# Attention tiles hold two heads of both batches of a pair: products g evicted over 128 rows, products h over two halves of 64 rows

## The chip, the core and the metric

One core of a Trainium2 chip. The metric is the device time of one execution in microseconds; the kernel before ran three times, with a median of 1440.73 (1438.68 to 1441.16). A further execution was profiled. TensorE multiplies (its weight loads are PEld in the profile), VectorE (DVE) and ScalarE (ACT) read its results from PSUM, which has eight banks, GpSimd (POOL) works on on-chip memory only, and SyncE (SP) issues all DMAs, in order.

## What is computed

Attention with 32 memory slots per head, then two MoE-like layers without routing:

```python
a = softmax over the sequence of phi                      # batch 8, heads 8, seq 576, slots 32
k_m, v_m = a^T k, a^T v                                   # per head: 32 x 64
attn = softmax over the slots of (q k_m^T / 8);  out = attn v_m
x = out, heads side by side                               # 4608 tokens x 512
h = max(x w1, x w2, x w3);  x2 = h w_out                  # w: 512 x 768, w_out: 768 x 512
y = (sigmoid(x2 w_gate) * (x2 w_val)) w_out2              # 512 x 1536 twice, 1536 x 512
```

## The kernel before

Every product is done with operands split into a rounded upper part and a remainder, in three passes (`PASSES`: low by high, high by low, high by high), to keep the precision.

*Pairs.* The batches are taken two at a time: pair `p` of four holds batches `2p` and `2p+1`. Attention works on groups of four heads of one batch (16 groups, `n`), in stages `a0` to `a5`: maximum and exponential of phi, transposes on TensorE (L193, L194), `k_m` and `v_m` (L207), transposes of those (L227; `a3` leaves the transposed `v_m` in `VT`), scores (L245), softmax, and `a_split`, which leaves the weights of the slots, 4 heads x 32 = 128 rows by 576 tokens, high and low, in `AT[n]`.

*Products g and h.* The output of attention is never formed. Since `x w = attn (v_m w)`, `g_step` multiplies `v_m` into a piece of the weights, and `h_step` multiplies the attention weights into that. `j` runs over six blocks of 128 of the 768 columns, `hp` over the four pairs of heads, `w` over w1, w2, w3. One `g_step(p, j, hp)` takes two heads of *both* batches: 128 rows come out, 32 for each head and batch, by 3 x 128 columns. An `h_step` wants the four heads of one batch in 128 rows, so `g_step` writes each half of its 64 rows to another tile, `G[b, j, g]`: two copies by ScalarE (the high part, L356) and two subtractions by VectorE (the low part, called in `sub`, L73) of 64 x 384 each. In pair 0, where `hp` is 0, ScalarE copies the product to `gf` first and GpSimd subtracts. `h_step(p, j, u)` then does 288 tokens of one batch (`u` from 0 to 3: batch `u // 2`, half `u % 2`): 18 matmuls over 128 rows into three PSUM banks (L369), a copy and two maxima (L379 to L381), and the high and low parts of `h`.

*x2.* `x2_step` multiplies all six blocks of `h` with `wo1` (L392), copies the result to a tile `x` of three buffers and stores it in DRAM (`x2s`).

*Order.* A loop over `s` sets it: 24 steps of `g_step(p, j+1, u)` and `h_step(p, j, u)`, then 16 of `x2_step`, with the next pair's attention stages spread over them by the spacing `a_st`. Into pair 0 the conversion and splitting of the first layer's weights is strewn (`w_step`: L122 to L126, `w_split` L131), into pairs 0 and 1 the conversion of the second layer's (`b_step`), into pair 3 sums and splits of those (`t_steps`, tiles `tb`) and of the first rows of the second layer (`x_load`, `x_sums`, `x_split`: tiles `xf`, `xa`). A scheduler then moves instructions on each engine. The second layer (L690, L757) follows; the change doesn't touch it.

Of the kernel before, what the change touches and what calls it, by code (L numbers as in the profile page):

```python
# [18 lines left out]
def attn_moe_kernel(  # L19
# [20 lines left out]
    U = S // 2  # L40
# [22 lines left out]
    def f32(ap):  # L63
        return ap.bitcast(F32)
# [69 lines left out]

    A = {}

    def early(shape):

        t = low.tile([128, 2 * U], F32R, tag="h", name="early", bufs=4 * J)
        return f32(t[:, :shape[1]])  # L140

    def load_phi(n):
        st = A[n] = {"kv": [], "q": []}
        if n in (2, 3):
            st["phi"] = early([128, S])
        else:
            st["phi"] = att.tile([128, S], F32, tag="phi", name="phi", bufs=2)
        dma(st["phi"], phiT[n])

    def load_kv(n):  # L150
        for c in range(5):
            if n < 4:
                t = early([128, 512])
            else:
                t = att.tile([128, 512], F32, tag="kv", name="kv", bufs=7)
            if c < 4:
                dma(t, kvm[n, c])
            else:
                dma(t[:64], kvt[n])
            A[n]["kv"].append(t)  # L160

    def load_q(n, e):
        if (n, e) in ((0, 0), (0, 1)):
            t = early([128, S])
        else:
            t = att.tile([128, S], F32, tag="q", name="q", bufs=3)
        dma(t, qT[n, e])
        A[n]["q"].append(t)


# [50 lines left out]

    def a3(n):
        st = A[n]
        b, g = divmod(n, 2)
# [6 lines left out]
        if b % 2 == 0:  # L231
            VT[b // 2, g] = mid.tile([128, 2, 4, 64], F32R, tag="vt", name="vt", bufs=4)
        vt = VT[b // 2, g]
        src = p[:, 128:256].rearrange("p (h m) -> p h m", h=2)
        for h in range(2):
            x = 3 * h if b % 2 == 0 else 2 - h
            act.copy(vt[:, 0, x], src[:, h])
            sub(vec, vt[:, 1, x], src[:, h], f32(vt[:, 0, x]))

    def a4(n):  # L240
        st = A[n]
# [90 lines left out]
    PASSES = ((1, 0), (0, 1), (0, 0))  # L332

    def g_step(p, j, hp):
        g, e = divmod(hp, 2)
        if e == 0:
            for b in range(2):
                G[b, j, g] = mid.tile([128, 2, 384], F32R, tag=f"g{b}", name=f"g{b}", bufs=3 + b)
        ps = bank()
        vt, w = VT[p, g], WX.pop((j, hp))  # L340
        for n, (x, y) in enumerate(PASSES):
            pe.matmul(  # L342
                ps[:, :384],
                lhsT=vt[:, x, 2 * e:2 * e + 2].rearrange("p a m -> p (a m)"),
                rhs=w[:, y],
                start=(n == 0), stop=(n == 2),
            )
        yield
        src, eng = ps, vec
        if p == 0 and hp == 0:  # L350
            src, eng = mid.tile([128, 384], F32, tag="gf", name="gf", bufs=1), pool
            act.copy(src, ps[:, :384])
        for hf in range(2):
            r = slice(64 * hf, 64 * hf + 64)
            t = G[(hf + e) % 2, j, g]
            act.copy(t[r, 0], ps[r, :384])  # L356
            sub(eng, t[r, 1], src[r, :384], f32(t[r, 0]))

    H = {}

    def h_step(p, j, u):
        b, hf = divmod(u, 2)
        ps = [bank() for _ in range(3)]
        for w in range(3):
            n = 0
            for g in range(2):
                at = AT[2 * (2 * p + b) + g]
                for x, y in PASSES:
                    pe.matmul(  # L369
                        ps[w][:, :U],  # L370
                        lhsT=G[b, j, g][:, x, 128 * w:128 * w + 128],
                        rhs=at[:, y, hf * U:hf * U + U],
                        start=(n == 0), stop=(n == 5),
                    )
                    n += 1
        yield
        h = mid.tile([128, U], F32, tag="hf", name="hf", bufs=2)
        m = mid.tile([128, U], F32, tag="hm", name="hm", bufs=2)
        act.copy(h, ps[0][:, :U])  # L379
        vec.tensor_tensor(out=m, in0=ps[1][:, :U], in1=h, op=ALU.max)  # L380
        vec.tensor_tensor(out=m, in0=ps[2][:, :U], in1=m, op=ALU.max)  # L381
        t = low.tile([128, 2 * U], F32R, tag="h", name="h", bufs=4 * J).rearrange("p (two t) -> p two t", two=2)
        H[u, j] = t
        copy(vec if u == 0 else act, t[:, 0], m)
        sub(pool, t[:, 1], m, f32(t[:, 0]))

    def x2_step(p, u, d):
        ps = bank()
        n = 0
        for j in range(J):  # L390
            for x, y in PASSES:
                pe.matmul(  # L392
                    ps[:, :U],
                    lhsT=wo1_t[:, x, (d * J + j) * 128:(d * J + j) * 128 + 128],
                    rhs=H[u, j][:, y],
                    start=(n == 0), stop=(n == 3 * J - 1),
                )
# [169 lines left out]
    for p in range(NP):  # L567
# [63 lines left out]
        for s in range(NS + NX):  # L631
            if last and s == NS:
                mid.release()
                b1 = tc.alloc_tile_pool(name="b1", bufs=1, side="right", reuse_waits="tile")
            gens = []
            for k, n in atts.get(s, ()):
                if len(atts[s]) > 1:
                    run(stages[k](n))
                    load_ahead(k, n)
                else:  # L640
                    gens.append(stages[k](n))
            if s < NS:
# [225 lines left out]
```

## Time and profile before

| | us |
|---|---|
| median of three runs | 1440.73 |
| the profiled execution | 1442.94 |
| its span | 1440.4 |
| TensorE busy (x7864 matmuls) | 1351.1 |
| VectorE, ScalarE, GpSimd busy | 843.7, 582.8, 545.8 |
| products g (L342), 37.5 to 524.9 | 71.7 busy |
| products h (L369), 51.3 to 536.8 | 258.2 busy |
| x2 (L392), 161.0 to 575.0 | 159.3 busy |
| second layer, first matmul | 608.5 |

The span is the time from the first to the last instruction of the profiled execution; its own device time is 2.5 us longer. Products h of pair 0 stand from 51 to 161, of pair 1 from 215 to 298, of pair 2 from 345 to 423, of pair 3 from 468 to 537, each followed by that pair's x2.

### The profile page before, as it was taken

To read this page: it belongs to the slowest core of one execution; us is meant where nothing else is said; L and a number is where in the kernel's file an instruction comes from. 1 tells how busy PE (TensorE), PEld (TensorE's weight loads), DVE (VectorE), ACT (ScalarE), POOL (GpSimd) and SP (SyncE) were. 2 spreads that over 40 slices of the span, in tenths; PEclk is the share of its full clock that TensorE was granted. 3 is DMA by queue.
4 is the path that set the end of the run, shared out by engine and by line. 5 is a ranking of instruction groups with operands and counts; after the bars stand their busy time and mean duration, and the time that the engine had idled before them with its cause. 6 is when DMAs were issued, how large, how long until landed. Compare 5 with 4: busy or idle time off the path is not lost.

```text
span 1440.4 us, 22273 instructions
## 1 busy us (share of the span) xinstructions
PE 1351.1 (94%) x7864; PEld 1187.6 (82%) x7864; DVE 843.7 (59%) x1508; ACT 582.8 (40%) x1236; POOL 545.8 (38%) x480
## 2 busy tenths in 40 slices
PE   6578899999999999199999999999999999999998
PEld 3477788889999999088888888888888899999997
DVE  5999979987754872334545445544355544454454
ACT  6668657756553662332223222242212422132221
POOL 3666512341344677921128211182112721161111
PEclk8789999999999999599999999999999999999999
DMA  9578799977636967874456644565444666566651
GB/s 306 197 249 290 263 308 329 305 274 262 187 91 238 402 251 288 323 295 147 159 178 216 205 146 146 171 213 200 151 149 156 218 233 225 184 232 220 222 204 72
DMA packets 120045, 320.75 MB, mean 223 GB/s; under 512 B 13440, under 2 KB 29824, under 8 KB 119936
## 3 DMA queue, kind: packets, MB, share of 16 engines
q1 hardware_dynamic: 119936, 319.35, 65.0%
q8 instruction: 62, 1.02, 0.3%
q14 instruction: 47, 0.39, 0.1%
HBM read 253.23 MB, written 66.06 MB: 222 GB/s over the span
## 4 chain that ended last, share of the span: by engine, by line
PE 74%; DVE 7%; DMA 7%; ACT 4%; issue 4%; POOL 3%; SPq 0%; DVEq 0%; POOLq 0%; ACTq 0%
PE po L757 21%; PE px L690 16%; PE pz L690 10%; PE pv L690 10%; PE ps L369 8%; PE ps L392 5%; DMA raw<-wb_dram 2%; DMA raw<-wx_dram 2%; PE ps L342 2%; DVE g L73 2%; DVE ca L126 1%; POOL tb L73 1%; DVE ca L124 1%; POOL xa L73 1%; ACT g L356 1%
## 5 line engine op out<-in xcount | busy, mean ns | idle before, releaser
L73 POOL TENSOR_TENSOR gg<-gf,gg 128x512 fp32r<-128x512 f32 (+1 forms) x120 | 142.4, 1186 | 556.1 <-ACT gg L723 556.1
L757 PE MATMUL po<-wo,gg 128*128 128x512 f32 x1296 | 332.8, 395 | 1.0 <-POOL gg L73 1.0
L757 PEld LDWEIGHTS po<-wo,gg 128*128 128x128 f32 x1296 | 242.6, 188 | 55.2 <-POOL gg L73 1.3
L690 PE MATMUL px<-xa,tb 128*128 128x512 f32 (+1 forms) x1080 | 248.0, 371 | 33.2 <-DMA tb<-tbs 33.2
L369 PE MATMUL ps<-attn,g 128*128 128x288 f32 x1728 | 258.2, 303 | 20.9 <-POOL s L73 7.0
L369 PEld LDWEIGHTS ps<-attn,g 128*128 128x128 f32 x1728 | 245.4, 193 | 30.8 <-POOL s L73 7.3
L690 PEld LDWEIGHTS px<-xa,tb 128*128 128x128 f32 x1080 | 199.8, 189 | 63.0 <-issue 33.4
L769 DVE TENSOR_TENSOR acc<-po,acc 128x512 f32<-128x512 f32 x180 | 124.4, 691 | 202.7 <-PE po L757 202.5
L690 PE MATMUL pv<-xa,tb 128*128 128x512 f32 (+1 forms) x720 | 170.3, 369 | 0.0
L690 PE MATMUL pz<-xa,tb 128*128 128x512 f32 (+1 forms) x720 | 170.0, 369 | 0.0
L392 PE MATMUL ps<-h,wo 128*128 128x288 f32 x1152 | 159.3, 297 | 0.0
L392 PEld LDWEIGHTS ps<-h,wo 128*128 128x128 f32 x1152 | 155.7, 190 | 1.9 <-issue 0.8
L741 DVE TENSOR_TENSOR u<-pz,p 128x512 f32<-128x512 f32 (+1 forms) x120 | 76.3, 636 | 131.4 <-PE pz L690 127.0
L690 PEld LDWEIGHTS pz<-xa,tb 128*128 128x128 f32 x720 | 132.6, 188 | 19.6
L723 ACT CAST gg<-gf 128x512 fp32r<-128x512 f32 (+1 forms) x120 | 69.5, 579 | 193.3 <-DVE gf L719 137.1
L690 PEld LDWEIGHTS pv<-xa,tb 128*128 128x128 f32 x720 | 131.8, 188 | 18.7
L73 POOL TENSOR_TENSOR h<-hm,h 128x288 fp32r<-128x288 f32 x96 | 87.6, 916 | 140.1 <-ACT h L68 83.5
L713 ACT ACTIVATE sg<-sg 128x512 f32<-128x512 f32 (+1 forms) x90 | 53.1, 590 | 163.2 <-DVE sg L711 163.0
L73 DVE TENSOR_TENSOR g<-ps,g 64x384 fp32r<-64x384 f32 x180 | 99.2, 551 | 26.2 <-ACT g L356 22.8
L356 ACT CAST g<-ps 64x384 fp32r<-64x384 f32 x192 | 90.9, 474 | 43.1 <-DVE g L73 21.9
L73 POOL TENSOR_TENSOR xa<-xf,xa 128x512 fp32r<-128x512 f32 (+1 forms) x70 | 84.9, 1239 | 29.9 <-ACT xa L131 29.7
L342 PE MATMUL ps<-wx,vt 128*128 128x384 f32 x288 | 71.7, 359 | 9.6 <-DVE vt L73 3.4
(87 smaller groups left out, 1398.5 us busy)
## 6 DMA issues: line engine op xcount, KB each, us to landing
tb<-tbs SPq DMA_DIRECT2D x210, 512.0 KB, 3.9
wo<-wos SPq DMA_DIRECT2D x60, 512.0 KB, 4.9
wx<-wxs SPq DMA_DIRECT2D x72, 384.0 KB, 5.2
tbs<-tb SPq DMA_DIRECT2D x42, 512.0 KB, 5.2
raw<-wb_dram SPq DMA_DIRECT2D x48, 384.0 KB, 4.9
kv<-kvm_dram SPq DMA_DIRECT2D x48, 256.0 KB, 4.4
raw<-wx_dram SPq DMA_DIRECT2D x24, 384.0 KB, 3.6
wxs<-wx SPq DMA_DIRECT2D x24, 384.0 KB, 5.2
```

Of the source, the lines that this page charges most:

```text
L73: eng.tensor_tensor(out=o, in0=a, in1=b, op=ALU.subtract)
L124: vec.tensor_scalar(out=ai, in0=ai, scalar1=3, scalar2=None, op0=ALU.logical_shift_left)
L342: pe.matmul(ps[:, :384], lhsT=vt[:, x, 2 * e:2 * e + 2].rearrange("p a m -> p (a m)"), rhs=w[:, y], start=(n == 0), stop=(n == 2),)
L356: act.copy(t[r, 0], ps[r, :384])
L369: pe.matmul(ps[w][:, :U], lhsT=G[b, j, g][:, x, 128 * w:128 * w + 128], rhs=at[:, y, hf * U:hf * U + U], start=(n == 0), stop=(n == 5),)
L392: pe.matmul(ps[:, :U], lhsT=wo1_t[:, x, (d * J + j) * 128:(d * J + j) * 128 + 128], rhs=H[u, j][:, y], start=(n == 0), stop=(n == 3 * J - 1),)
L690: pe.matmul(ps[:, :half], lhsT=w[:, a, o:o + 128], rhs=x[:, k, c, :half], start=(first and n == 0), stop=(n == 5), skip_group_check=not first,
L713: act.activation(out=sg, in_=src, func=AF.Sigmoid)
L723: act.copy(t[:, 0, :half], gf)
L741: vec.tensor_tensor(out=u, in0=ps[:, :half], in1=E["p1", v], op=ALU.add)
L757: pe.matmul(ps, lhsT=GG[sc, j, c, h][:, x, 128 * m:128 * m + 128], rhs=WO[sc, j, h][:, y], start=(n == 0), stop=(n == 5),)
L769: vec.tensor_tensor(out=t, in0=ps, in1=t, op=ALU.add)
```

## The change

Attention groups are cut otherwise: group `n = 4p + hp` holds two heads of batch `2p` in rows 0 to 63 and the same two heads of batch `2p+1` in rows 64 to 127 (`source` says where they stand in the inputs, which keep their layout). The rows of attention weights, of `v_m` and of a product g are now in the same order, so `a3` copies `v_m` whole, and `g_step` evicts its 128 rows with one copy and one subtraction into one tile `G[j, hp]`, always by ScalarE and VectorE. An `h_step` now does one half of the tokens for both batches: 72 matmuls over 64 rows each, which alternate between the lower half of the rows (batch 0) and the upper (batch 1), into six PSUM banks. The `h` tiles hold both batches (576 columns), their upper part is always copied by ScalarE, and the number of h steps per `j` is two instead of four. Loads of phi, k and v come in two pieces per group, one for each batch; k and v in runs of 256 numbers instead of 512. `x` has two buffers instead of three.

```diff
+    def source(n, b):
+        p, hp = divmod(n, 4)
+        g, pr = divmod(hp, 2)
+        return 2 * (2 * p + b) + g, pr ^ b
...
-        dma(st["phi"], phiT[n])
+        for b in range(2):
+            m, pr = source(n, b)
+            dma(st["phi"][64 * b:64 * b + 64], phiT[m, 64 * pr:64 * pr + 64])
...
+            for b in range(2):
+                m, pr = source(n, b)
+                dma(t[:, :, 256 * b:256 * b + 256],
+                    kvm[m, c:c + 2, :, 256 * pr:256 * pr + 256].rearrange("c s x -> s c x"))
...
     def a3(n):
...
-        for h in range(2):
-            x = 3 * h if b % 2 == 0 else 2 - h
-            act.copy(vt[:, 0, x], src[:, h])
-            sub(vec, vt[:, 1, x], src[:, h], f32(vt[:, 0, x]))
+        vt = VT[n] = mid.tile([128, 2, 128], F32R, tag="vt", name="vt", bufs=8)
+        act.copy(vt[:, 0], p[:, 128:256])
+        sub(vec, vt[:, 1], p[:, 128:256], f32(vt[:, 0]))
...
     def g_step(p, j, hp):
...
-        src, eng = ps, vec
-        if p == 0 and hp == 0:
-            src, eng = mid.tile([128, 384], F32, tag="gf", name="gf", bufs=1), pool
-            act.copy(src, ps[:, :384])
-        for hf in range(2):
-            r = slice(64 * hf, 64 * hf + 64)
-            t = G[(hf + e) % 2, j, g]
-            act.copy(t[r, 0], ps[r, :384])
-            sub(eng, t[r, 1], src[r, :384], f32(t[r, 0]))
+        t = G[j, hp] = mid.tile([128, 2, 384], F32R, tag="g", name="g", bufs=8)
+        act.copy(t[:, 0], ps[:, :384])
+        sub(vec, t[:, 1], ps[:, :384], f32(t[:, 0]))
...
-    def h_step(p, j, u):
-        b, hf = divmod(u, 2)
-        ps = [bank() for _ in range(3)]
+    def h_step(p, j, hf):
+        ps = [[bank() for _ in range(2)] for _ in range(3)]
         for w in range(3):
             n = 0
-            for g in range(2):
-                at = AT[2 * (2 * p + b) + g]
+            for hp in range(4):
+                at = AT[4 * p + hp]
                 for x, y in PASSES:
-                    pe.matmul(
-                        ps[w][:, :U],
-                        lhsT=G[b, j, g][:, x, 128 * w:128 * w + 128],
-                        rhs=at[:, y, hf * U:hf * U + U],
-                        start=(n == 0), stop=(n == 5),
-                    )
+                    for b in range(2):
+                        r = slice(64 * b, 64 * b + 64)
+                        pe.matmul(
+                            ps[w][b][:, :U],
+                            lhsT=G[j, hp][r, x, 128 * w:128 * w + 128],
+                            rhs=at[r, y, hf * U:hf * U + U],
+                            start=(n == 0), stop=(n == 11),
+                        )
                     n += 1
         yield
-        h = mid.tile([128, U], F32, tag="hf", name="hf", bufs=2)
-        m = mid.tile([128, U], F32, tag="hm", name="hm", bufs=2)
-        act.copy(h, ps[0][:, :U])
-        vec.tensor_tensor(out=m, in0=ps[1][:, :U], in1=h, op=ALU.max)
-        vec.tensor_tensor(out=m, in0=ps[2][:, :U], in1=m, op=ALU.max)
...
-        copy(vec if u == 0 else act, t[:, 0], m)
+        m = mid.tile([128, 2, U], F32, tag="hm", name="hm", bufs=2)
+        for b in range(2):
+            act.copy(m[:, b], ps[0][b][:, :U])
+        for w in (1, 2):
+            for b in range(2):
+                vec.tensor_tensor(out=m[:, b], in0=ps[w][b][:, :U], in1=m[:, b], op=ALU.max)
...
+        act.copy(t[:, 0], m)
         sub(pool, t[:, 1], m, f32(t[:, 0]))
...
-        t = low.tile([128, U], F32, tag="x2", name="x2", bufs=3)
+        t = low.tile([128, U], F32, tag="x2", name="x2", bufs=2)
...
-                gens.append(h_step(p, j, u))
+                if u % 2 == 0:
+                    gens.append(h_step(p, j, u // 2))
```

What stands on TensorE in the middle of pair 2's products h, before: L342 is a product g, L369 products h (`g_` tiles are its weights), L193 and L194 transposes of attention.

```order
L342 MATMUL ps<-wx,vt 128x384 x3
L369 MATMUL ps<-attn,g_4776 128x288 x9
L193 MATMUL ps<-ident,et 128x128 x4
L194 MATMUL ps<-ident,et 64x128
L369 MATMUL ps<-attn,g_4890 128x288 x9
```

And in the changed kernel, from the end of pair 1's x2 (L407) into pair 2: L359 is g, L381 h, L219, L220 and L233 attention.

```order
L407 MATMUL ps<-h,wo_82 128x288 x90
L359 MATMUL ps<-wx,vt 128x384 x3
L381 MATMUL ps<-attn,g 128x288 x72
L219 MATMUL ps<-ident,et 128x128 x4
L220 MATMUL ps<-ident,et 64x128
L359 MATMUL ps<-wx,vt 128x384 x3
L233 MATMUL ps<-kv,es 32x128 x16
L233 MATMUL ps<-kvt,es 32x128 x4
```

The h matmuls, 64 rows each, now stand in one block of 72, with g, attention or x2, which use other tilings of the array, on both sides.

VectorE in pair 0 where the first maximum stands, before (`hm` is the maximum, `g_` a product g's low part, `ca` a weight's conversion in three steps):

```order
L126 SCALAR_TENSOR_TENSOR ca<-raw,ca 128x384
L125 ISA ca<-ca,cr 128x768
L73 TENSOR_TENSOR g_654<-ps,g_654 64x384
L380 TENSOR_TENSOR hm<-ps,hf 128x288
L271 TENSOR_SCALAR sm<-sm 128x18
```

The same place in the changed kernel:

```order
L73 TENSOR_TENSOR g<-ps,g 128x384
L124 TENSOR_SCALAR ca<-ca 128x384
L125 ISA ca<-ca,cr 128x768
L124 TENSOR_SCALAR ca<-ca 128x384
L126 SCALAR_TENSOR_TENSOR ca<-raw,ca 128x384
L125 ISA ca<-ca,cr 128x768
L126 SCALAR_TENSOR_TENSOR ca<-raw,ca 128x384
L394 TENSOR_TENSOR hm<-ps,hm 128x288
```

One subtraction of 128 rows stands where two of 64 stood, and 14 conversions (L126) are ahead of the first maximum instead of nine.

GpSimd at the end of pair 3's products h, before: `tb` are the second layer's weights, `xa` its rows.

```order
L73 TENSOR_TENSOR tb<-td,tb 128x512
L73 TENSOR_TENSOR tb<-tw,tb 128x512
L73 TENSOR_TENSOR tb<-two,tb 128x512 x2
L73 TENSOR_TENSOR h<-hm,h 128x288 x2
L73 TENSOR_TENSOR tb<-tw,tb 128x512
L73 TENSOR_TENSOR h<-hm,h 128x288
L73 TENSOR_TENSOR xa<-xf,xa 128x512
```

And in the changed kernel:

```order
L73 TENSOR_TENSOR tb<-td,tb 128x512
L73 TENSOR_TENSOR tb<-tw,tb 128x512
L73 TENSOR_TENSOR tb<-two,tb 128x512 x2
L73 TENSOR_TENSOR h<-hm,h 128x576
L73 TENSOR_TENSOR tb<-tw,tb 128x512
L73 TENSOR_TENSOR h<-hm,h 128x576 x6
L73 TENSOR_TENSOR xa<-xf,xa 128x512
```

All 37 pieces `tb` that stood among or ahead of pair 3's pieces of h still do, and 17 still follow; the last six pieces of h now come together.

More of the change, by code (lines that the diff above doesn't have):

```diff
@@ L135, in attn_moe_kernel, with early_tile, early @@
     A = {}
-    def early(shape):
-        t = low.tile([128, 2 * U], F32R, tag="h", name="early", bufs=4 * J)
-        return f32(t[:, :shape[1]])
+    halves = []
+    def early_tile():
+        return f32(low.tile([128, 4 * U], F32R, tag="h", name="early", bufs=2 * J))
+    def early(cols):
+        if not halves:
+            t = early_tile()
+            halves.extend((t[:, :2 * U], t[:, 2 * U:]))
+        return halves.pop(0)[:, :cols]
+    def source(n, b):
+        p, hp = divmod(n, 4)
+        g, pr = divmod(hp, 2)
+        return 2 * (2 * p + b) + g, pr ^ b
     def load_phi(n):
@@ L144, in load_phi @@
         if n in (2, 3):
-            st["phi"] = early([128, S])
+            st["phi"] = early(S)
         else:
             st["phi"] = att.tile([128, S], F32, tag="phi", name="phi", bufs=2)
-        dma(st["phi"], phiT[n])
+        for b in range(2):
+            m, pr = source(n, b)
+            dma(st["phi"][64 * b:64 * b + 64], phiT[m, 64 * pr:64 * pr + 64])
     def load_kv(n):
-        for c in range(5):
+        for c in (0, 2):
             if n < 4:
-                t = early([128, 512])
+                t = early_tile()[:, :1024]
             else:
[L155 to L160, printed above, removed]
+                t = att.tile([128, 1024], F32, tag="kv", name="kv", bufs=3)
+            t = t.rearrange("p (c x) -> p c x", c=2)
+            for b in range(2):
+                m, pr = source(n, b)
+                dma(t[:, :, 256 * b:256 * b + 256],
+                    kvm[m, c:c + 2, :, 256 * pr:256 * pr + 256].rearrange("c s x -> s c x"))
+            A[n]["kv"] += [t[:, 0], t[:, 1]]
+        if n < 4:
+            t = early(512)
+        else:
+            t = att.tile([128, 512], F32, tag="kvt", name="kvt", bufs=1)
+        for b in range(2):
+            m, pr = source(n, b)
+            dma(t[:64, 256 * b:256 * b + 256], kvt[m, :, 256 * pr:256 * pr + 256])
+        A[n]["kv"].append(t)
     def load_q(n, e):
         if (n, e) in ((0, 0), (0, 1)):
-            t = early([128, S])
+            t = early(S)
         else:
             t = att.tile([128, S], F32, tag="q", name="q", bufs=3)
-        dma(t, qT[n, e])
+        m, pr = source(n, e)
+        dma(t, qT[m, pr])
         A[n]["q"].append(t)
@@ L223, in a3 @@
         st = A[n]
-        b, g = divmod(n, 2)
         p = bank()
@@ L230, in a3 @@
         act.copy(kt, p[:, 0:128])
[L231 to L234, printed above, removed]
-        for h in range(2):
-            x = 3 * h if b % 2 == 0 else 2 - h
-            act.copy(vt[:, 0, x], src[:, h])
-            sub(vec, vt[:, 1, x], src[:, h], f32(vt[:, 0, x]))
+        vt = VT[n] = mid.tile([128, 2, 128], F32R, tag="vt", name="vt", bufs=8)
+        act.copy(vt[:, 0], p[:, 128:256])
+        sub(vec, vt[:, 1], p[:, 128:256], f32(vt[:, 0]))
     def a4(n):
@@ L334, in g_step @@
     def g_step(p, j, hp):
[L335 to L338, printed above, removed]
         ps = bank()
-        vt, w = VT[p, g], WX.pop((j, hp))
+        vt, w = VT[4 * p + hp], WX.pop((j, hp))
         for n, (x, y) in enumerate(PASSES):
@@ L343, in g_step @@
                 ps[:, :384],
-                lhsT=vt[:, x, 2 * e:2 * e + 2].rearrange("p a m -> p (a m)"),
+                lhsT=vt[:, x],
                 rhs=w[:, y],
@@ L375, in h_step @@
                     n += 1
         yield
-        h = mid.tile([128, U], F32, tag="hf", name="hf", bufs=2)
-        m = mid.tile([128, U], F32, tag="hm", name="hm", bufs=2)
-        act.copy(h, ps[0][:, :U])
-        vec.tensor_tensor(out=m, in0=ps[1][:, :U], in1=h, op=ALU.max)
-        vec.tensor_tensor(out=m, in0=ps[2][:, :U], in1=m, op=ALU.max)
-        t = low.tile([128, 2 * U], F32R, tag="h", name="h", bufs=4 * J).rearrange("p (two t) -> p two t", two=2)
-        H[u, j] = t
-        copy(vec if u == 0 else act, t[:, 0], m)
+        m = mid.tile([128, 2, U], F32, tag="hm", name="hm", bufs=2)
@@ L385, in h_step @@
+        for b in range(2):
+            act.copy(m[:, b], ps[0][b][:, :U])
+        for w in (1, 2):
+            for b in range(2):
+                vec.tensor_tensor(out=m[:, b], in0=ps[w][b][:, :U], in1=m[:, b], op=ALU.max)
+        t = low.tile([128, 4 * U], F32R, tag="h", name="h", bufs=2 * J)
+        t = t.rearrange("p (two b t) -> p two b t", two=2, b=2)
+        H[hf, j] = t
+        act.copy(t[:, 0], m)
         sub(pool, t[:, 1], m, f32(t[:, 0]))
     def x2_step(p, u, d):
+        b, hf = divmod(u, 2)
@@ L394, in x2_step @@
                     lhsT=wo1_t[:, x, (d * J + j) * 128:(d * J + j) * 128 + 128],
-                    rhs=H[u, j][:, y],
+                    rhs=H[hf, j][:, y, b],
                     start=(n == 0), stop=(n == 3 * J - 1),
```

## The prediction

> **What bounds the kernel now.** I read the page first, then busy time by stage, the groups of instructions with shapes kept apart, and the order of time on TensorE.
>
> ```profile
> span 1440.4 us, 22273 instructions
> PE 1351.1 (94%) x7864; PEld 1187.6 (82%) x7864; DVE 843.7 (59%) x1508; ACT 582.8 (40%) x1236; POOL 545.8 (38%) x480
> ```
>
> The span, and each engine's busy time: read alone, it says that TensorE is everything. The stages say more. Columns: stretch, its length, then busy time and count of each engine, granted clock, DMA share, GB/s.
>
> ```profile
> 0.00:37.00 37.00, 22.92 (x215) 11.33 (x216) 19.88 (x49) 22.69 (x57) 11.82 (x17) 0.82 0.93 305
> 37.00:52.00 15.00, 5.80 (x25) 3.79 (x24) 14.94 (x25) 11.18 (x26) 11.12 (x10) 0.84 0.63 222
> 52.00:110.00 58.00, 45.04 (x240) 41.91 (x239) 54.06 (x95) 39.21 (x89) 35.54 (x33) 0.81 0.69 224
> 110.00:161.00 51.00, 44.57 (x366) 39.27 (x364) 47.96 (x100) 41.20 (x100) 32.26 (x31) 1.00 0.78 267
> 161.00:214.00 53.00, 48.92 (x406) 45.52 (x404) 45.37 (x95) 29.65 (x70) 13.77 (x12) 0.97 0.92 308
> 214.00:344.00 130.00, 125.61 (x1014) 117.34 (x1012) 118.14 (x261) 89.00 (x212) 40.48 (x36) 1.00 0.89 301
> 344.00:475.00 131.00, 131.00 (x1074) 125.56 (x1073) 80.97 (x170) 68.20 (x161) 50.47 (x48) 1.00 0.57 190
> 475.00:575.00 100.00, 99.66 (x724) 97.94 (x723) 61.10 (x113) 52.57 (x113) 75.16 (x66) 1.00 0.82 308
> 575.00:609.00 34.00, 0.77 (x4) 0.56 (x3) 11.85 (x8) 10.86 (x19) 32.72 (x26) 0.57 0.87 310
> ```
>
> From 37 to 161 (pair 0, products h) VectorE is the bound: 14.94 + 54.06 + 47.96 = 117 of 124 us. Pair 1 (214 to 344) has TensorE at 125.6 of 130 with VectorE close behind, pair 2 TensorE at 131 of 131. Pair 3's TensorE is full too, but its work is followed by 34 us in which GpSimd alone is busy (32.7): the way into the second layer is GpSimd's. Everything after 609 the change leaves alone. So relief of VectorE pays in pair 0, extra TensorE time costs in pairs 1 and 2, and in pair 3 it meets a slack that I look for below.
>
> **The prices.**
>
> ```profile
> L369 PE MATMUL ps<-attn,g 128*128 128x288 f32 x1728 | 258.2, 303 | 20.9 <-POOL s L73 7.0 <-DVE g L73 3.8 <-ACT hf L379 3.7
> L73 DVE TENSOR_TENSOR g<-ps,g 64x384 fp32r<-64x384 f32 x180 | 99.2, 551 | 26.2 <-ACT g L356 22.8
> L711 DVE TENSOR_TENSOR sg<-px,u 128x384 f32<-128x384 f32 x12 | 6.6, 554 | 1.4 <-PE px L690 1.4
> L356 ACT CAST g<-ps 64x384 fp32r<-64x384 f32 x192 | 90.9, 474 | 43.1 <-DVE g L73 21.9 <-PE ps L342 17.7
> L70 DVE CAST h<-hm 128x288 fp32r<-128x288 f32 x24 | 11.3, 469 | 0.2
> L73 POOL TENSOR_TENSOR h<-hm,h 128x288 fp32r<-128x288 f32 x96 | 87.6, 916 | 140.1 <-ACT h L68 83.5 <-DVE h L70 48.5 <-PE ps L342 6.3
> L73 POOL TENSOR_TENSOR attn<-stg,attn 128x576 fp32r<-128x576 f32 x16 | 23.7, 1485 | 14.4 <-ACT attn L283 14.3
> L73 POOL TENSOR_TENSOR g<-gf,g 64x384 fp32r<-64x384 f32 x12 | 13.3, 1108 | 2.0 <-ACT g L356 1.6
> ```
>
> Rows two and three: 384 columns take VectorE 551 ns over 64 rows and 554 over 128, so evicting g once over 128 rows halves its cost. Now TensorE around two changes of its tiling (the 128*128 is the tile; 128*64 and 128*32 are column tiles of the attention):
>
> ```profile
> 217.21 0.60 PE L193 MATMUL ps<-ident,et 128*128 128x128 f32 x4
> 217.64 0.27 PE L194 MATMUL ps<-ident,et 128*64 128x128 f32 x1
> 350.87 1.43 PE L207 MATMUL ps<-kv,es 128*32 128x128 f32 x40
> 352.24 0.81 PE L342 MATMUL ps<-wx,vt 128*128 128x384 f32 x3
> 352.88 2.54 PE L369 MATMUL ps<-attn,g 128*128 128x288 f32 x18
> 358.92 1.34 PE L369 MATMUL ps<-attn,g 128*128 128x288 f32 x9
> 360.20 1.19 PE L245 MATMUL ps<-q,kt 128*64 128x288 f32 x8
> 361.32 1.46 PE L369 MATMUL ps<-attn,g 128*128 128x288 f32 x9
> 362.61 0.68 PE L342 MATMUL ps<-wx,vt 128*128 128x384 f32 x3
> 363.13 2.56 PE L369 MATMUL ps<-attn,g 128*128 128x288 f32 x18
> 365.53 0.69 PE L342 MATMUL ps<-wx,vt 128*128 128x384 f32 x3
> 366.05 2.53 PE L369 MATMUL ps<-attn,g 128*128 128x288 f32 x18
> ```
>
> Starts tell the rate (ends are modelled): 18 matmuls of h from 363.13 to 365.53, 133 ns each.
>
> *Products h.* 1728 matmuls over 128 rows become 3456 over 64, alternating between the lower and the upper half of the rows, which no row of this trace does. The nearest rows are column tiles: L207's 40 matmuls of 128 columns take 1.37 us, 34 ns each, where the full array takes 108 ns for 128 columns (L193, 0.43 us for four). Four column tiles thus run side by side, and I take the same for two row tiles: a pair for the price of one, 133 ns, change 0. The other end is a turn each, another 133 ns on each of 1728 pairs (rivals).
>
> *Changes of tiling.* Each block of h now lies between matmuls of the full array. Counted in the two orders, pairs 0 to 3 get 28, 23, 21 and 22 more changes of tiling. Nine matmuls of h take 1.19 us at 133 ns; before a change they take 360.20 − 358.92 = 1.28, after one 362.61 − 361.32 = 1.29; three of g take 0.64 (352.24) against 0.52 (365.53). So 0.09 to 0.12 us a change is seen; the wait for the first hidden weight load in the new tiling adds up to 0.11 (the 108 ns of L193). Ends 0.09 and 0.22; I take 0.17, near the upper end, because h and g both load 128 columns. Pairs 1 and 2: 44 × 0.17 = +7.5 us (4 to 10), with nothing to hide them. Pair 0's 28 lie under VectorE. The Trainium skill ("TensorEngine Tiling (Array Packing)", Key Properties) says that switching the mode drains TensorE, and names no price. The trace agrees; with nothing for the drain the sum below would be −8.0, with the rows it is −0.5.
>
> *Evicting g, pair 0.* VectorE loses 36 × 551 = 19.8 us (18 of 24 steps; GpSimd had the other six) and gets 24 × 554 = 13.3, and loses 6 casts of h at 469 = 2.8: 9.3 us less in a stage that it fills to 94%. The six GpSimd steps (13.3 us in all) and their copies go too. Ends: −13, if also its waits behind GpSimd shrink, and +2, if the new order eats it. I take −8. Covered elsewhere: in pairs 1 to 3 the same relief (about 16 us each) lies on engines that are not the bound; of pair 1's 4.4 us of TensorE idling I give −2 (0 to −4).
>
> *The first h.* It needs all four attention tiles now, not two.
>
> ```profile
> 51.27 2.50 PE L369 MATMUL ps<-attn,g 128*128 128x288 f32 x9 [6.98 <-POOL s L73]
> 72.67 1.61 POOL L73 TENSOR_TENSOR attn<-stg,attn 128x576 fp32r<-128x576 f32 x1
> ```
>
> The fourth tile was ready at 74.3 in the old order, h started at 51.3. Counted in the new order, VectorE has five subtractions of g ahead of that tile's last step instead of eleven, and four maxima and a cast less (6 × 0.55 + 4 × 0.45 + 0.47 = 5.6 us); GpSimd loses two of g just before it (2.2). So I expect it near 66, and VectorE does weight conversions meanwhile (14 instead of 9 before the first maximum). Work is exchanged, not lost: 0, and this is the ground of a rival.
>
> *PSUM.* h takes six banks at a time instead of three of eight. A bank comes round after g, h and what attention lies between; the last maxima (2 × 0.45 us) have g's 2 × 0.52 us and the next first third of h (24 × 133 / 2 = 1.6 us) to get done. 0 to +4, taken 0, under VectorE's relief.
>
> *x2 with two buffers instead of three.*
>
> ```profile
> DVE x L70: 20.8, 6
> DMA to landing us min/median/max: 1.7/3.4/7.2
> ```
>
> A copy waits for the store two before it: 0.46 + 3.4 us per two steps is 1.9 a step at the median, below a step's 18 × 133 = 2.4; at 7.2 it is 3.8. These waits exist already (20.8 us on VectorE), eight banks stand between them and TensorE, but ScalarE and VectorE queue attention behind them. 0 to +8, taken +2.
>
> *Loads.* phi, k and v come in more and shorter DMAs: eight more issues on SP among the first four tiles, all ahead of the first weights in the queue; DMA stood at 0.93 of its engines then. +1 (0 to 3).
>
> *Pair 3.*
>
> ```profile
> 537.13 9.34 PE ps L392 x71
> 546.00 0.81 POOL L73 TENSOR_TENSOR h<-hm,h 128x288 fp32r<-128x288 f32 x1
> 546.48 7.22 DMA xf<-x2s
> 601.85 6.54 DMA tb<-tbs
> ```
>
> TensorE ends h at 537.1, yet GpSimd's last piece of h comes at 546.0, behind 37 subtractions tb, and only then the second layer's rows load; 17 tb stay behind it in both orders. h costs GpSimd 24 × 0.916 = 22 us now and 12 × 1.485 = 17.8 then. TensorE's 22 × 0.17 = 3.7 fit into the 9 us. −1 (−4 to +4).
>
> **Sum:** +7.5 − 8 − 2 + 0 + 2 + 1 − 1 = −0.5 us against the profiled execution (1442.9 us, span 1440.4 and 2.5 around it). That execution lies 2.2 above the median of the runs, 1440.7; so 1440.2, I say **1440**: no change.
>
> **Rivals.** *A turn each:* the two halves don't overlap. Pairs 1 and 2: 864 × 133 = 115 us; pair 3: 57 + 4 − 9 = 52; pair 0: h doubles to 115 us of TensorE, with g and attention some 135 from 66 on, ending near 200 instead of 161: about +40. About 1645. For it: no row shows row tiles together; against it: L207. It decides early: 3 ns more per exposed pair is already 2.6 us. Chance 0.12.
>
> *Loads a turn each:* products overlap, weight loads don't. A load of 128 columns is bounded by L193 at 108 ns; two are 216, 83 more than 133: pairs 1 and 2 +72, pair 3 +31, pair 0 about +20, near 1563. Against it: L207 needs a load per matmul, and 34 ns each leaves no room for turns of column tiles. Chance 0.08. The Trainium skill ("TensorE: Matmul & The Clock Gate", LDWEIGHTS) says that a load takes P/1.2 ns for P columns whatever the number of rows: an estimate of 107 ns for each half. The trace's 108 agrees; with 107, turns would give an estimated 1561.
>
> *Pair 0 gives nothing:* the late first h eats VectorE's relief; −8 becomes 0: 1448. For it: VectorE was 94% busy either way; chance 0.20. *Pair 0 gives all:* −13, pair 1 −4, x2 and loads near 0: 1430 to 1434; chance 0.20.
>
> **Numbers.** Likeliest 0.40, its own range 1435 to 1446. Faster by over 0.2% (2.9 us, about what a measurement of this kernel can tell from no change): 0.20 + 0.14 = 0.34. Within: 0.20 + 0.02 = 0.22. Slower: 0.06 + 0.18 + 0.20 = 0.44. The range leaves out the two turn-taking cases: 1427 (all gains) to 1460 (all of x2, PSUM and changes at their ends).
>
> **What would show it.** Right: the new h row with 3456 matmuls in about 230 to 260 us busy, blocks of 72 what follows them starting some 4.8 us after them; pair 2 longer by 3 to 5 us; pair 0's h ending near 150; VectorE near 785 us busy; GpSimd's tail still 70 us long. Wrong: blocks of 72 taking 8 or 9.6 us; TensorE waiting for the maxima in pairs 1 and 2; x2 copies waiting long on stores with TensorE idle behind them.

## The result, and the profile after

The changed kernel takes 1545.64 us (1543.58 to 1547.85, four runs), the kernel before 1440.43: 1.0733 times as long, 95% interval 1.0714 to 1.0751. The forecast, 1440 with a range to 1460, missed it by 106 us. The experiments show that something the forecast had taken as given cost some 108 us: the order of the instructions on VectorE and ScalarE. In another order the same instructions take 1436.35 us, near the forecast, though by terms that cancel.

The page of after, span and busy time:

```profile
span 1546.1 us, 25295 instructions
PE 1402.3 (91%) x9592; PEld 1214.0 (79%) x9592; DVE 780.0 (50%) x1384; ACT 531.1 (34%) x1094; POOL 513.2 (33%) x420
```

VectorE lost 64 us (843.7 to 780.0; 785 was forecast). TensorE's row of h has its 3456 matmuls, but is 280 us busy where 230 to 260 were forecast. By stages (columns as in the prediction):

```profile
37.00:52.00 15.00, 12.48 (x67) 7.76 (x63) 14.25 (x27) 10.60 (x25) 10.73 (x9) 0.78 0.68 227
52.00:110.00 58.00, 36.20 (x297) 31.08 (x299) 38.41 (x72) 26.61 (x58) 21.93 (x19) 0.71 0.63 207
110.00:161.00 51.00, 34.91 (x368) 28.57 (x365) 34.68 (x70) 29.68 (x69) 21.52 (x19) 0.83 0.68 217
161.00:214.00 53.00, 37.52 (x357) 32.23 (x357) 40.51 (x81) 26.12 (x60) 10.02 (x8) 0.81 0.80 253
214.00:344.00 130.00, 101.81 (x960) 90.22 (x960) 88.31 (x188) 64.79 (x151) 23.58 (x17) 0.87 0.82 267
344.00:475.00 131.00, 127.06 (x1409) 116.60 (x1410) 54.91 (x127) 46.34 (x110) 31.88 (x24) 0.97 0.47 147
```

From 52 to 161 VectorE works 73 of 109 us (102 before), and no other engine is full either. No engine bounds pairs 0 and 1 any more; they wait for one another. The granted clock fell with it, to 0.71 and 0.83 where it had been 0.81 and 1.00. In times of TensorE's first and last matmul: pair 0's products h end at 209.7 (160.7 before), pair 1's last 118.0 us (83.4), pair 2's 82.0 (78.4), pair 3's 87.9 (69.5); the second layer starts at 713.8 (608.5).

Who waits for whom from 37 to 400 us (columns: total, times, longest): VectorE before, then VectorE after,

```profile
DVE nm L180 <- DMA phi<-phiT_dram: 0.6, 1, 0.6
```

```profile
DVE ca L124 <- ACT ca L122: 32.5, 29, 3.1
DVE nm L206 <- DMA phi<-phiT_dram: 25.7, 9, 7.5
DVE g L73 <- ACT g L367: 18.0, 17, 3.2
```

ScalarE before, then after,

```profile
ACT ca L122 <- DMA raw<-wb_dram: 29.1, 21, 3.3
```

```profile
ACT ca L122 <- DMA raw<-wb_dram: 64.9, 32, 7.0
```

and TensorE after, from 37 to 720:

```profile
PE ps L381 <- DVE hm L394: 25.9, 14, 4.7
PE ps L381 <- DVE g L73: 22.7, 9, 3.7
PE ps L233 <- ACT es L223: 22.1, 4, 7.5
```

One such wait, from the timeline of after: VectorE, ScalarE and TensorE.

```profile
79.39 1.65 DVE L126 SCALAR_TENSOR_TENSOR ca<-raw,ca 128x384 uint32<-128x384 uint32 x1
85.89 0.75 DVE L206 TENSOR_REDUCE nm<-phi 128x1 f32<-128x576 f32 x1 [4.84 <-DMA phi<-phiT_dram]
87.57 0.15 DVE L211 TENSOR_SCALAR rs<-ss 128x1 f32<-128x1 f32 x1 [0.93 <-ACT et L209]
87.84 1.53 DVE L394 TENSOR_TENSOR hm<-ps,hm 128x288 f32<-128x288 f32 x4
```

```profile
81.48 0.68 ACT L391 COPY hm<-ps 128x288 f32<-128x288 f32 x2
```

```profile
81.92 1.75 PE L381 MATMUL ps<-attn,g 64*128 64x288 f32 x18 [2.00 <-ACT hm L391]
88.33 1.21 PE L381 MATMUL ps<-attn,g 64*128 64x288 f32 x5 [4.66 <-DVE hm L394]
91.51 5.01 PE L381 MATMUL ps<-attn,g 64*128 64x288 f32 x49 [1.97 <-DVE g L73]
```

VectorE's next instruction is the maximum of a later group's phi, whose load has not landed. VectorE stands still for 4.84 us, and so do the four maxima of h behind that instruction, though ScalarE's copies, with which they compare, were there at 82.2; TensorE stops inside a block of h for 4.66 us, since those maxima have not freed its banks. The Trainium skill ("TensorE: Matmul & The Clock Gate", Architectural detail) says that the queues of ScalarE and VectorE are strictly first in, first out, while TensorE's can pull weight loads ahead. These rows agree for VectorE.

So which instructions stand ahead of h matters. Counted on VectorE, the conversions of weights (L126, one of each three instructions of a conversion) ahead of pair 0's last maximum, and ahead of the maximum that ends the first third of pair 1, are 34 and 54 in the kernel before, 49 and 78 in the changed one. The fifth reduction of phi, the one in the rows above, stands behind 12 maxima of h before and behind 4 after. The piece of VectorE's order after the change that the wait above belongs to (the first number is the place in that order, repeats counted once):

```
102 L126 SCALAR_TENSOR_TENSOR ca<-raw,ca 128x384
103 L206 TENSOR_REDUCE nm<-phi 128x1
104 L211 TENSOR_SCALAR rs<-ss 128x1
105 L212 RECIPROCAL rs<-rs 128x1
106 L394 TENSOR_TENSOR hm<-ps,hm 128x288 x4
107 L73 TENSOR_TENSOR g<-ps,g 128x384 x2
```

The conversions were done at about the old times (27 of them from 37 to 161, where 28 were done before). So it was not more work that delayed products h, but having been put behind that work; e7 and e10 below test this.

### The profile page after: what moved, and what is told of

It reads as the page before. It is cut to its first block, busy times and chain, and to the rows that moved or that the text cites. A ratio compares the mean times of both kernels' runs of the same rounds, so it can differ in the third digit from the quotient of the medians.

```text
span 1546.1 us, 25295 instructions
## 1 busy us (share of the span) xinstructions
PE 1402.3 (91%) x9592; PEld 1214.0 (79%) x9592; DVE 780.0 (50%) x1384; ACT 531.1 (34%) x1094; POOL 513.2 (33%) x420
## 4 chain that ended last, share of the span: by engine, by line
PE 71%; DMA 11%; DVE 4%; POOL 3%; ACT 2%; issue 2%; SPq 1%; ACTq 0%; DVEq 0%; POOLq 0%
PE po L773 20%; PE px L706 15%; PE pz L706 10%; PE pv L706 10%; PE ps L381 8%; PE ps L407 5%; DMA raw<-wb_dram 5%; PE ps L359 2%; DVE ca L126 1%; POOL tb L73 1%; DMA wx<-wxs 1%; PE ps L233 1%; DMA phi<-phiT_dram 1%; DMA tw<-wbf 1%; POOL xa L73 1%
## 5 line engine op out<-in xcount | busy, mean ns | idle before, releaser
L381 PE MATMUL ps<-attn,g 64*128 64x288 f32 x3456 | 280.2, 315 | 62.1 <-DVE hm L394 25.9
L381 PEld LDWEIGHTS ps<-attn,g 64*128 64x128 f32 x3456 | 259.6, 202 | 85.1 <-DVE hm L394 31.2
L407 PE MATMUL ps<-h,wo 128*128 128x288 f32 x1152 | 160.8, 298 | 0.0
L407 PEld LDWEIGHTS ps<-h,wo 128*128 128x128 f32 x1152 | 156.4, 190 | 2.9 <-issue 2.7
L73 POOL TENSOR_TENSOR h<-hm,h 128x576 fp32r<-128x576 f32 x48 | 69.7, 1453 | 254.4 <-ACT h L398 254.4
L706 PEld LDWEIGHTS pz<-xa,tb 128*128 128x128 f32 x720 | 132.7, 188 | 19.7
L394 DVE TENSOR_TENSOR hm<-ps,hm 128x288 f32<-128x288 f32 x192 | 77.7, 448 | 57.3 <-PE ps L381 49.2
L73 DVE TENSOR_TENSOR g<-ps,g 128x384 fp32r<-128x384 f32 x96 | 52.9, 554 | 58.0 <-ACT g L367 57.9
L359 PE MATMUL ps<-wx,vt 128*128 128x384 f32 x288 | 72.2, 373 | 5.6 <-DVE g L73 2.0
```

What stands on the lines that cost most here:

```text
L73: eng.tensor_tensor(out=o, in0=a, in1=b, op=ALU.subtract)
L359: pe.matmul(ps[:, :384], lhsT=vt[:, x], rhs=w[:, y], start=(n == 0), stop=(n == 2),)
L381: pe.matmul(ps[w][b][:, :U], lhsT=G[j, hp][r, x, 128 * w:128 * w + 128], rhs=at[r, y, hf * U:hf * U + U], start=(n == 0), stop=(n == 11),)
L394: vec.tensor_tensor(out=m[:, b], in0=ps[w][b][:, :U], in1=m[:, b], op=ALU.max)
L407: pe.matmul(ps[:, :U], lhsT=wo1_t[:, x, (d * J + j) * 128:(d * J + j) * 128 + 128], rhs=H[hf, j][:, y, b], start=(n == 0), stop=(n == 3 * ...
L706: pe.matmul(ps[:, :half], lhsT=w[:, a, o:o + 128], rhs=x[:, k, c, :half], start=(first and n == 0), stop=(n == 5), skip_group_check=not first,
```

## Experiments

The numbers are those by which the expectations name them (there is no e5). Measured are the median and its ratio to the kernel before, with the 95% interval. Theories: ORDER (above); PSUM (six banks at a time leave too little slack); LOADS (shorter, more DMAs); ROWS (products over 64 rows have a cost of their own).

### e1. Full-array products h in the changed kernel

```diff
-                    for b in range(2):
-                        r = slice(64 * b, 64 * b + 64)
-                        pe.matmul(
-                            ps[w][b][:, :U],
-                            lhsT=G[j, hp][r, x, 128 * w:128 * w + 128],
-                            rhs=at[r, y, hf * U:hf * U + U],
-                            start=(n == 0), stop=(n == 11),
-                        )
+                    b = n // 6
+                    pe.matmul(
+                        ps[w][b][:, :U],
+                        lhsT=G[j, hp][:, x, 128 * w:128 * w + 128],
+                        rhs=at[:, y, hf * U:hf * U + U],
+                        start=(n % 6 == 0), stop=(n % 6 == 5),
+                    )
```

> The changed kernel with products h as 36 matmuls over all 128 rows (six into each of the six banks) instead of 72 over 64 rows; tiles, banks, loads, evictions and the order written stay. It mixes the two batches, so only its time is read. ORDER (leading theory): the scheduler puts 49 conversions of weights (L126) ahead of the last maximum of pair 0 in the changed kernel, 34 in the kernel before, and 78 against 54 by a third of pair 1; products h wait behind them on VectorE and ScalarE. In this kernel the counts are again 34 and 54, so pair 0's products h end near 160 us, pair 1's pair near 300, and the time is 1425 to 1450. PSUM (rival): six of eight banks are still taken at a time, so TensorE still waits for evictions; only the changes of tiling go (some 100 x 0.19 us at most): 1525 to 1540. LOADS (rival): smaller loads are kept: 1525 to 1540.

Measured: 1433.72 us, 0.9952 (0.9936 to 0.9968) of the kernel before. Six banks, one eviction of g, shorter loads and two buffers for x together are no loss. Either the row tiles or the order did it, and both went here.

### e2. The loads of before in the changed kernel

```diff
-        for b in range(2):
-            dma(st["phi"][64 * b:64 * b + 64], phiT[m, 64 * pr:64 * pr + 64])
+        dma(st["phi"], phiT[n])
...
-                t = att.tile([128, 1024], F32, tag="kv", name="kv", bufs=3)
+                t = att.tile([128, 512], F32, tag="kv", name="kv", bufs=7)
```

> The changed kernel with the loads of the kernel before: phi in one DMA for a group, k and v in runs of 512 numbers, seven buffers for k and v. The groups then hold four heads of one batch, so only its time is read. LOADS (rival): VectorE waited 25.7 us for phi in the changed kernel between 37 and 400 us and 0.6 before, ScalarE 64.9 for raw weights against 29.1; if the smaller loads are the cause, both go back and the time is 1440 to 1470. ORDER and PSUM: the waits stay, since the conversions ahead of h are counted 48 and 78 here too and the banks are the same: 1535 to 1555.

Measured: 1519.98, 1.0559 (1.0544 to 1.0575). Neither expectation: 26 us come back, 80 stay. VectorE still waits for phi (18.5 us in place of 25.7). So the loads are not the main cause, and e1 kept them without harm. Whether the 26 us are theirs alone is not shown, since the order moved a little too (16 conversions ahead of the first maximum, where the changed kernel has 14).

### e3. Six banks at a time in the kernel before

```diff
-        ps = [bank() for _ in range(3)]
+        ps = [[bank() for _ in range(2)] for _ in range(3)]
...
-                gens.append(h_step(p, j, u))
+                if u % 2 == 0:
+                    gens.append(h_step(p, j, u // 2))
```

> The kernel before with products h done two halves at a time: every second step, 36 matmuls over 128 rows into six banks, evicted as in the changed kernel (two copies, four maxima, one copy and one subtraction of 576 columns). Nothing else changes; the output is the reference's. PSUM (rival): six banks of eight and evictions in lumps are the cause, so TensorE waits for maxima as in the changed kernel: 1500 to 1540. ORDER: the conversions ahead of h are counted 35 and 55, as in the kernel before: 1430 to 1450.

Measured: 1465.04, 1.0183 (1.0166 to 1.0200): between the two. What TensorE mostly waits for there is not the maxima (L386) but g (37 to 400 us):

```profile
PE ps L373 <- DVE g L73: 18.1, 13, 3.5
PE ps L373 <- DVE hm L386: 4.4, 5, 2.3
```

With the old double eviction, a block of h every second step follows straight on the last g that it needs. Banks or bunching, these 25 us were not taken apart further; in e1, with one eviction of g, the six banks cost nothing that shows.

### e4. Conversions held back in the changed kernel

```diff
+    def kept_back(ins):
+        if not queue["in order"]:
+            tc.keep_in_program_order(ins)
...
-        act.activation(out=a, in_=hi.bitcast(F32), func=AF.Abs, scale=DOWN)
+        kept_back(act.activation(out=a, in_=hi.bitcast(F32), func=AF.Abs, scale=DOWN))
```

(and the same for L123 and L124)

> The changed kernel with each conversion of weights (its two instructions on ScalarE and its first on VectorE) held behind everything that is written ahead of it on its engine. 26 conversions then stand ahead of pair 0's last maximum (49 in the changed kernel) and 42 by a third of pair 1 (78). The output is the reference's. ORDER: TensorE's waits for maxima and g go in pairs 0 and 1; pair 0's products h end near 155 to 165, pair 1's are 85 long; what is left is the changes of tiling (7 to 12) and conversions that come later: 1430 to 1460. PSUM and LOADS: banks and loads are the changed kernel's: 1520 to 1550.

Measured: 1510.84, 1.0503 (1.0483 to 1.0524). 35 us come back, too few for ORDER as I had put it. The wait has moved to what was not held:

```profile
DVE nm L210 <- DMA phi<-phiT_dram: 43.2, 8, 8.1
```

So conversions are a part; the attention stages that run ahead of h look like another.

### e6. The changed kernel in the order of e1, three queues held

Edit, here and below: at the kernel's end each instruction of a queue is tied behind the one that stands ahead of it in a table of positions, which is read off another program. Nothing else changes.

```diff
+    for name, text in ORDER_OF.items():
+        own = [i for i in nc.cur_bb.bb.instructions if str(i.engine).endswith("." + name) ...]
+        row = [int(x) for x in text.split()]
...
+        for a, b in zip(row, row[1:]):
+            tc.add_manual_dep(own[b], own[a].name, ...)
```

> The changed kernel, word for word, but VectorE, GpSimd and the DMA queue are made to take their instructions in the order that they had in the experiment with full-array products h (1433.7 us): 34 conversions ahead of pair 0's last maximum instead of 49, 54 by a third of pair 1 instead of 78. ScalarE and TensorE are left free. The output is the reference's. ORDER: what the changed kernel lost was its order; only the changes of tiling are left, at most 94 x 0.19 = 18 us, of which pairs 1 and 2 give 8.4 for certain: 1442 to 1455. ROWS (rival): products over 64 rows bring waits or a slower clock of their own, whatever the order: 1480 to 1540.

Measured: 1511.28, 1.0492 (1.0470 to 1.0515). This spoke for ROWS. But ScalarE had been left free.

### e7. The mirror: full-array products in the changed kernel's order

```diff
+    ORDER_OF = {"DVE": ..., "Activation": ..., "Pool": ..., "SP": ...}
```

(the edit of e6, on the kernel of e1)

> The other way round: the kernel with full-array products h (1433.7 us) with VectorE, ScalarE, GpSimd and the DMA queue in the order of the changed kernel. No row tiling is in it; it mixes the two batches, so only its time is read. ORDER: the order alone costs what the changed kernel lost, less the changes of tiling: 1515 to 1540. ROWS: without products over 64 rows it stays fast: 1434 to 1460.

Measured: 1541.80, 1.0694 (1.0678 to 1.0710). Without a single row tile, order alone costs 108.1 us (1541.8 − 1433.7; the kernel before read 2.0 us higher beside e7 than beside e1, so some 106 to 108). Of that, 96 us are lost by the end of pair 1's x2. Pair 3's h takes 15 us more than in e1, of which the way into the second layer gives 9 back; which instructions stand badly there is not shown. The waits are like those of the changed kernel, TensorE's from 37 to 720 and VectorE's from 37 to 400 us:

```profile
PE ps L380 <- DVE hm L393: 34.3, 17, 5.3
```

```profile
DVE nm L206 <- DMA phi<-phiT_dram: 25.9, 9, 7.2
```

Row tiles add 3.8 us to that (1545.6). ROWS is out as the cause of the loss; why e6 stayed slow was now the question.

### e8. Two buffers for x in the kernel before

```diff
-        t = low.tile([128, U], F32, tag="x2", name="x2", bufs=3)
+        t = low.tile([128, U], F32, tag="x2", name="x2", bufs=2)
```

> The kernel before with two buffers for x instead of three, and nothing else. The prediction took +2 us for it (0 to +8); the experiment with full-array products has two as well and ran at 1433.7, which speaks for little. ORDER: the conversions ahead of h are 34 and 54, as before: 1438 to 1446. BUFFERS (rival: copies of x2 that wait for stores hold VectorE and ScalarE): 1448 to 1480.

Measured: 1448.00, 1.0048 (1.0033 to 1.0063): +6.7 us, near the upper end of the prediction's 0 to +8.

### e9. h on odd steps, three queues held

```diff
-                if u % 2 == 0:
+                if u % 2 == 1:
                     gens.append(h_step(p, j, u // 2))
```

> The changed kernel with each h step moved one step later (u = 1 and 3 instead of 0 and 2), so that a block of h stands between the last g of a block j and the first h that needs it, and with VectorE, GpSimd and the DMA queue in the order that the same program gets with full-array products (33 and 54 conversions at the two places). The output is the reference's. ORDER: as e6, less the waits of h for the eviction of the last g (about 0.5 us in some of 24 blocks): 1436 to 1452, the first version of row tiling that may stand level with the kernel before. ROWS: 1475 to 1540.

Measured: 1516.20, 1.0523 (1.0502 to 1.0543), and TensorE waits nearly only for ScalarE, the one queue left free:

```profile
PE ps L252 <- ACT kvb L243: 40.4, 11, 7.8
```

### e10. All four queues held

```diff
+    ORDER_OF = {"DVE": ..., "Activation": ..., "Pool": ..., "SP": ...}
```

(the edit of e6, on the changed kernel; the order is that of e11)

> The changed kernel, word for word, with VectorE, ScalarE, GpSimd and the DMA queue in the order that the scheduler gives the same program when its products h are 36 matmuls over 128 rows, alternating between the two banks as the 72 do (the next kernel). 31 conversions then stand ahead of pair 0's last maximum, 51 by a third of pair 1, and TensorE's order is the same too. The output is the reference's. ORDER, with ScalarE's order as the part that e6 left out (there ScalarE waited 76.7 us for raw weights, 39.7 with full-array products): the time is that of the next kernel plus 4 (what the changed kernel has over e7) to 18 us (94 changes of tiling x 0.19): 1438 to 1455. ROWS (rival): products over 64 rows have a cost of their own that shows only when nothing else holds them, and e6 measured it: 1490 to 1515.

Measured: 1436.35, 0.9976 (0.9965 to 0.9987). The changed kernel, with no instruction added or taken away, is 109 us faster than it was, and a little faster than the kernel before. From 37 to 161 us:

```profile
37.00:110.00 73.00, 63.16 (x637) 53.52 (x638) 67.72 (x127) 51.09 (x117) 43.01 (x34) 0.90 0.80 259
110.00:161.00 51.00, 47.55 (x568) 42.31 (x565) 46.55 (x93) 32.70 (x77) 26.38 (x21) 1.00 0.85 278
```

VectorE is full again (114 of 124 us), TensorE has gone through 1205 matmuls where it had 732, and the clock is back at 0.90 and 1.00. Between 52 and 161 us TensorE stood idle four times for 4.66 to 5.72 us in the changed kernel; here its longest gaps are 4.36 and 2.42. The Trainium skill ("TensorE: Matmul & The Clock Gate", HAM oscillation) says that idle gaps of TensorE beyond some 3.4 us bring its clock down. These stages agree with it; from 161 to 214 of the changed kernel the clock was 0.81 with no gap above 3.37 us, just under that figure. The phi maximum that stood ahead of four maxima of h now stands behind them, and behind 16 maxima in all:

```
113 L394 TENSOR_TENSOR hm<-ps,hm 128x288 x2
114 L126 SCALAR_TENSOR_TENSOR ca<-raw,ca 128x384
115 L124 TENSOR_SCALAR ca<-ca 128x384
116 L394 TENSOR_TENSOR hm<-ps,hm 128x288 x2
...
120 L73 TENSOR_TENSOR g<-ps,g 128x384
121 L125 ISA ca<-ca,cr 128x768
122 L206 TENSOR_REDUCE nm<-phi 128x1
```

### e11. The program that lent the order

```diff
-                    b = n // 6
+                    b = n % 2
```

(on the kernel of e1, with `start` and `stop` to match, so that both banks of a `w` fill together)

> Full-array products h as 36 matmuls, alternating between the two banks of a w, otherwise the changed kernel; its order is the one that e10 copies. It mixes the batches, so only its time is read. ORDER and ROWS both: as with six in a row into one bank, 1430 to 1442; both banks of a w finish together here, some 0.8 us later than the first did there, which may cost up to 5.

Measured: 1427.25, 0.9902 (0.9885 to 0.9920). In the same order, row tiles cost 9.1 us (1436.35 − 1427.25). Pair 2's products h take 78.6 us here and 82.2 in e10: 3.6 us for the 19 more changes of tiling in that stretch, 0.19 each.

### e12. h on odd steps, all four queues

The edits of e9 and e10 together.

> As e10, with each h step one step later (u = 1 and 3), and the four orders copied from full-array products with the same step moved. e9 had only three of the four orders and waited 40.4 us for ScalarE at the transposes of k_m (L252). The output is the reference's. ORDER: those waits go and no h waits for the last g: 1436 to 1452. ROWS: 1490 to 1520.

Measured: 1449.59, 1.0058 (1.0035 to 1.0082). Those 40 us of waits fell to 18.1, but the odd steps gain nothing: the first h starts 4.7 us later than in e10 (50.5 against 45.8) and pair 1's h takes 88.6 instead of 84.6.

### e13. ScalarE alone left free

```diff
-    ORDER_OF = {"DVE": ..., "Activation": ..., "Pool": ..., "SP": ...}
+    ORDER_OF = {"DVE": ..., "Pool": ..., "SP": ...}
```

> As e10, from the same model of an order, but ScalarE left to the scheduler (VectorE, GpSimd and the DMA queue stay held). ScalarE then has 32 conversions ahead of its last copy of h in pair 0 where e10 has 30, one or two more nearly everywhere: a conversion's first instruction waits on ScalarE for its raw weights, and the copies of g and h stand behind it. SCALAR (leading): these one or two places are what kept e6 at 1511; 1490 to 1515. MODEL (rival): e6 was slow since its model had six matmuls in a row into one bank, and pairs end together here: 1436 to 1446.

Measured: 1515.82, 1.0517 (1.0500 to 1.0534): 79 us for one queue's order, in which it differs by 1.1 places on the average and 12 at most. ScalarE waits for raw weights, first here, then in e10 (37 to 400 us):

```profile
ACT ca L122 <- DMA raw<-wb_dram: 76.7, 33, 6.7
```

```profile
ACT ca L122 <- DMA raw<-wb_dram: 37.1, 22, 5.3
```

and behind it VectorE waits for ScalarE's copies of g (25.7 us, 12.0 in e10). ScalarE has 33 conversions ahead of its last copy of h in pair 0 here and 31 in e10, and one of them can wait up to 6.7 us for its data at the head of the queue. That these two make the loss fits the waits, but no run moved them alone.

### e14. VectorE and ScalarE alone held

```diff
-    ORDER_OF = {"DVE": ..., "Activation": ..., "Pool": ..., "SP": ...}
+    ORDER_OF = {"DVE": ..., "Activation": ...}
```

> As e10, but only VectorE and ScalarE are held in the copied order; GpSimd and the DMA queue are left to the scheduler (they end within 0.3 places of it on the average, 13 at most). SCALAR: these two queues carry the loss: 1434 to 1445. LOADS (rival): the order of the loads on the DMA queue carries a part: 1450 to 1500.

Measured: 1439.44, 0.9997 (0.9986 to 1.0009). To hold these two queues is enough. The other two, left to the scheduler, then come out in nearly the same order and cost some 3 us; what the changed kernel's own order of loads would cost is not shown.

### e15 and e16. Three buffers for x

```diff
-        t = low.tile([128, U], F32, tag="x2", name="x2", bufs=2)
+        t = low.tile([128, U], F32, tag="x2", name="x2", bufs=3)
...
-            t = mid.tile([128, 2, PC], F32R, tag="wx", name="wx", bufs=6)
+            t = mid.tile([128, 2, PC], F32R, tag="wx", name="wx", bufs=5)
```

(e15; in e16 it is `ca` that gives way, from three buffers to two. Both are edits of e10, each in the order of full-array products with the same buffers.)

> As e10, with three buffers for x again, paid for by five instead of six for the weights wx, and the order copied from full-array products with the same buffers. The output is the reference's. BUFFERS: two buffers for x cost the kernel before 6.7 us, so this gains some of that: 1429 to 1435. If wx's sixth buffer was needed (it is loaded again for every pair): 1438 to 1450.

> As e10, with three buffers for x again, paid for by two instead of three for a conversion's result ca, and the order copied from full-array products with the same buffers. The output is the reference's. BUFFERS: 1429 to 1435. If the third ca let a conversion's DMA to memory hide: 1440 to 1455.

Measured: 1429.54, 0.9925 (0.9905 to 0.9944), and 1447.06, 1.0042 (1.0025 to 1.0059). The first beats both kernels, by 0.75% the one before. With two buffers for `ca` more is lost than the third for x gives; VectorE's order also lies 4.3 places from that of e10 there (0.5 in e15), so buffers and order are not told apart.

### Where the order comes from

In the changed kernel the scheduler's order is almost that of a program with 72 products h over all 128 rows. There is no run of that program, only its order: its instructions stand 0.1 places from the changed kernel's on VectorE and ScalarE, on the average, with the same 49 and 78 conversions. The 36 products of e1 put VectorE's 13.9 places elsewhere. So the number of products sets the order, not their rows. The likely reason is that the scheduler reckons each 64-row product as a full one, expects products h to take twice what they take, and fills the time with conversions and attention stages of later groups; which durations it works with is not shown. On the chip the pairs overlap, and the h that came early stands behind that work.

## Why the prediction was wrong

*The step that failed* is "The first h". It noted 14 conversions instead of 9 before the first maximum, called it work exchanged, "0", and stopped counting there. The fourth tile came at 64.1 us, near the 66 foretold, yet the first maximum ran only at 72.8 (58.7 before, 65.5 in e10). Further on the count runs to 49 against 34 and 78 against 54, and reductions of phi slipped ahead of maxima. Both kinds wait for DMAs (in after, from 37 to 400 us, VectorE 25.7 us for phi and ScalarE 64.9 for raw weights), and h waits behind them. The whole sum took the waits of the old order and put the new durations on it. Measured: +108 us for order alone (e7), and 109 taken back by order alone (e10). The rival that this step was the ground of was priced at 8 us, and no other held it, so the range ended at 1460.

*Relief of VectorE in pair 0*, −8 (−13 to +2). In e10's order pair 0's x2 ends at 194.8 instead of 214.5, −19.7, beyond the good end; but that order also has 31 conversions ahead of pair 0's last maximum. In e1, with 34 as before, it ends at 203.8, −10.7 and inside the range. So the relief was about right in size, and the rest goes with the order.

*Changes of tiling*, +7.5 in pairs 1 and 2 at 0.17 each. About right in price: 0.19 in pair 2 (e10 against e11; two of the 21 counted for that pair lie in its x2). Wrong in place: pair 3's are not hidden, since the way into the second layer moved with them. From pair 2 to the second layer row tiles cost 9.0 us (h of pair 2 starts at 328.0 and 327.6, the second layer at 598.8 and 589.3), and pairs 0 and 1 together swallowed all but 0.4 us of theirs.

*Two halves for the price of one*, 0. Right; both turn-taking rivals fall. In pair 1 of after, a block of 72 and what follows it:

```profile
365.02 5.03 PE L381 MATMUL ps<-attn,g 64*128 64x288 f32 x72
369.97 0.79 PE L359 MATMUL ps<-wx,vt 128*128 128x384 f32 x3
```

4.95 us, where 36 x 133 ns are 4.8 and turns would need 8 or 9.6.

*PSUM*, 0 to +4. The Trainium skill ("TensorEngine Tiling (Array Packing)", Gotcha 1) warns of pressure on the banks from row tiles. TensorE's waits for maxima in after look like it (25.9 us), and I took them for it at first. In a good order the six banks go with 1427.25 and 1436.35 us: the pressure was the late maxima, not the number of banks. For the kernel before it remains open (e3).

*x2 with two buffers*, +2 (0 to +8): 6.7 (e8), under-sized, inside the range. I weighed the median landing of a store, which is 3.5 us in e8 and was 3.4 before; VectorE's and ScalarE's waits for stores rise from 20.8 to 35.5 us all the same, the longest 9.8.

*Loads*, +1: without visible harm in a good order (e1). In the bad one, the old loads took 26 us off (e2), not freed from the order.

*The sum*, 1440, describes the changed kernel in a proper order (1436.35), but as a sum of errors that cancel: pairs 0 and 1 cheaper, pair 3 and x2 dearer. That the total fits is luck.

## What to carry to other kernels

When a scheduler orders the queues, a change in the number or shape of instructions can also change the time that the scheduler expects of them: count the order at several places along the affected stages, not only at the first, and ask of each engine's queue what stands ahead of the instruction that frees another engine. In queues that are taken in order, an instruction that waits for a DMA costs all that is behind it, so an order of ScalarE that lies 1.1 places away on the average was worth 79 us here. And before a cause is sought in the new instructions, run the old ones in the new order and the new ones in the old.

## What was unexpected of the hardware

Matmuls over the upper and the lower 64 rows overlap entirely at 288 columns: in pair 2 the two of a pair start 3 to 4 ns apart (e10 and after), pairs 133 ns apart, the rate of one full-array matmul (133 ns in e11). A change of tiling costs 0.19 us where nothing else hides it (pair 2, e10 against e11).
